# Attention and expert layer on one core: another start order, rows in a ring, one store to a slot

## The chip, the cores and the metric

The kernel runs on one core of one Trainium2 chip. The metric is the device time of one execution in microseconds (us), as the median of several runs. The engines are TensorE (PE, with its weight loads shown as PEld), VectorE (DVE), ScalarE (ACT), GpSimd (POOL) and SyncE (SP), which here only issues DMAs. TensorE's clock can be throttled; the profile shows the granted share.

## The reference

Two stages follow each other. The first is a gated linear attention over 768 steps for 4 batches of 8 heads, with head size 48; the second is an expert layer with 8 experts, of which each token uses one.

```python
f = 1.0 / (1.0 + np.exp(-f_logit))
for t in range(S):
    state = f[:, :, t, :, None] * state + np.einsum('bhd,bhe->bhde', k[:, :, t], v[:, :, t])
    y[:, :, t] = np.einsum('bhd,bhde->bhe', q[:, :, t], state)
...
x = attn_out.transpose(0, 2, 1, 3).reshape(B * S, H * D)      # 3072 tokens of 384
logits = x @ w_gate
expert_idx = np.argmax(logits, axis=1)
...                                                            # tokens go to their expert's rows in order
h = np.maximum(np.einsum('ecd,edf->ecf', disp, w1), 0.0)
y = np.einsum('ecf,efd->ecd', h, w2)
out[i] = gate_w[i] * y[expert_idx[i], pos[i]]
```

## The kernel before, in words

The 3072 tokens are 24 blocks of 128 (`NT`), six to a batch. Attention runs as a software pipeline over slots: slot n, from -4 to 24, issues on every engine the instructions that belong to several blocks at once. The order on all five engines is written out by hand here (`tc.manual_schedule`): each engine's queue holds its instructions in the order in which `slot` issues them, and an instruction that waits holds up what is behind it on its engine. Ahead of the slots stand constants and the first loads, which a planner orders.

For block n the steps are, with the lines of the profile:

- `load` (L198 to L217): DMAs of f, of k and q (one each, to two halves of the partitions of one tile), and of v. One load of f serves two blocks; "f 2" below is the load for blocks 4 and 5. k and q have three buffers, f three, v six.
- `sig(u)` (L344, ACT): the sigmoid of load u of f into `pf`. `sig(0)` is in two parts.
- `f_in` (L353, PE): transposes of `pf` into `psF`. `decay` and `decay_back` (L373 to L387, DVE): two scans over it, `Suf` and `Rq`.
- `kq_pad` (L394 on POOL, L396 on ACT from slot 7 on): copies k and q into a padded tile `kqp`. `kq_in` (L353, PE, then L402, DVE): transposes into `psT`, and the products with `Suf` and `Rq`, called `kT` and `qT`.
- `scores_pe` (L413, PE) and `scores_out` (L419, ACT, then L421, POOL): scores, their copy into `AT`, and the causal mask.
- `keys_pe` (L438, PE) and `keys_out` (L444, ACT): keys transposed back (`kn`). The last block of a batch has none.
- `inter` (L455), `update` (L475), `values` (L509): products with the carried state, for the state, and for the output. `state` (DVE) and `carry` (L495, POOL) make the next state `S`.
- `rows_pe` (L530, PE), `rows_copy` (L542, ACT) and `rows_parts` (L553, ACT): output rows of 384 values and parts of the eight logits, by a product with `identc`, which holds an identity and the gate weights. A row has 393 columns: values, logits and the token's number, which POOL copies in (L538). `rows` is a tile of six blocks with two buffers.

In slot 0 the sigmoid of f 2 stands ahead of the copies of block 1's scores on ACT. `update` takes its PSUM bank from the pool `psA` of two, in which both halves of the scores lie until ACT has copied them.

Choosing the expert and ranking go by groups of blocks (six, six, three, three, three, one, one, one). When a group is ranked, its blocks join `queue`, and `flush_scatter` issues one indirect DMA on POOL (L313) that stores the 128 rows of one block to `disp`, in HBM. A slot has two places for it: ahead of `update`, and behind `carry`; `SCATTERS` says how many a slot does (2 where it isn't listed). Blocks up to 14 are early: their rows of the first expert are loaded as `xg0` at the end of slot 19 (L930) and used from L708 on. From slot 5 on the first expert's weights are loaded and split in pieces between the attention's instructions; the experts' products (L744, L996, L1169) follow.

`keep_busy(m)` (L363) issues m products of the identity, whose result nobody reads: 10 ahead of the slots, 3 in slot -3, 7 in slot -2. The small constants are collected with `put_off` and made on POOL in slot -3 (L814). `late_constants` issues five small DMAs, the gate weights into `identc` and the capacity (L269, L270).

Of the kernel before, what the change touches and what calls it, by code (L numbers as in the profile page):

```python
# [28 lines left out]
def kernel(  # L29
# [45 lines left out]
    QUARTERS = {9: (0, 3), 12: (0, 1), 13: (1, 2), 14: (1, 2), 18: (2, 1), 19: (2, 1), 20: (2, 2)}  # L75
    SCATTERS = {9: 1, 10: 2, 11: 2, 12: 1, 15: 2, 16: 2, 17: 2, 18: 2, 19: 1, 20: 0}
    PAD_ACT = 7
# [135 lines left out]

    for nm, n in (("f", 0), ("kq", 0), ("f", 1), ("kq", 1), ("v", 0), ("kq", 2), ("f", 2)):
        load(nm, n)
        if (nm, n) == ("kq", 0):
            nc.sync.dma_start(loads["f", 0].rearrange("t h j d -> t h (j d)")[64:], pairs("f", 1, C))  # L217
# [18 lines left out]
    def put_off(op, *args, **kw):  # L236
        put_off_ops.append((op, args, kw))

    identc = const.tile([P, NP, XW], F32, name="identc")
    put_off(nc.gpsimd.memset, identc, 0.0)  # L240
# [15 lines left out]
    desc = const.tile([P, NE], F32, name="desc")  # L256
    put_off(nc.gpsimd.tensor_copy, desc, desc_i)
    tok_i = const.tile([P, N // C], I32, name="tok_i")
    put_off(nc.gpsimd.iota, tok_i, pattern=[[C, N // C]], base=-TOK0, channel_multiplier=1)
# [5 lines left out]
    def late_constants():  # L265
        gates_of = w_gate.rearrange("(a b s d) e -> b s d a e", b=2, s=2, d=D)
        for g in range(2):
            for b in range(2):
                nc.sync.dma_start(identc[64 * g : 64 * g + D, b::2, 2 * D :], gates_of[b, g ^ b])  # L269
        nc.sync.dma_start(cap_i, capacity.bitcast(I32).partition_broadcast(P))  # L270
    ohc = const.tile([P, NE], BF16, name="ohc")
# [133 lines left out]
    MS = (64, D)  # L405
    pus, ATs, kns, pys, yTs, marks, rows_of, parts_of = {}, {}, {}, {}, {}, {}, {}, {}

# [8 lines left out]
    def scores_out(n, pas):  # L416
        AT = abuf.tile([P, 2, NP, C], F32, name="AT")
        for s in range(2):
            nc.scalar.activation(AT[:, s], pas[s], AF.Copy)  # L419
# [104 lines left out]
    def rows_pe(n):  # L524
# [7 lines left out]
        return px  # L532

    def row_at(n):
        t, c = divmod(n, RT)
        if t not in rows_of:
            rows_of[t] = abuf.tile([P, RT, W], F32, name="rows")
            nc.gpsimd.tensor_copy(rows_of[t][:, :, DM + NE : W], tokid[:, n : n + RT].unsqueeze(2))  # L538
        return rows_of[t][:, c]

    def rows_copy(n, px):
        m = nc.scalar.activation(  # L542
            row_at(n)[:, :DM].rearrange("r (a d) -> r a d", a=NP), px[:, :, : 2 * D], AF.Copy
        )
        if n >= NT - 5:
            flush_scatter()
        marks[n].append(m)
# [7 lines left out]
    def group(g, m):  # L555
        t, c = divmod(g, RT)
        return parts_of[t][:, c : c + m], rows_of[t][:, c : c + m, DM : DM + NE]

# [21 lines left out]
    def sum_parts(g, m):  # L580
        t, c = divmod(g, RT)
        nc.vector.tensor_reduce(
            out=rows_of[t][:, c : c + m, DM : DM + NE],
            in_=parts_of[t][:, c : c + m].rearrange("r c a e -> r c e a"),
# [90 lines left out]

    def flush_scatter():
        if queue:
            n = queue.pop(0)
            late = n >= SPLIT
            ins = scatter(disp, ri_of.pop(n), row_at(n), NV * RPE - 1, ("disp", "late") if late else ("disp",))  # L680
            if not late:
                early_ins[:] = [ins]


# [85 lines left out]
    def loads_of(n):  # L770
        if n == -3:
            load("kq", 3)
            load("v", 1)
        elif n == -2:
            load("kq", 4)
            late_constants()
        elif n == -1:
            load("v", 2)
            load("f", 3)
            load("kq", 5)  # L780
        elif n >= 0:
# [11 lines left out]
    def slot(n):  # L793
# [16 lines left out]
        if fn and n < PAD_ACT:  # L810
            kq_pad(n + 3)
        while n == -3 and put_off_ops:
            op, args, kw = put_off_ops.pop(0)
            op(*args, **kw)  # L814
        while half:
# [5 lines left out]
        if n == -2:  # L821
            keep_busy(7)
        if n % 2 and fn and n not in (-3, 1, 9, 15):
# [21 lines left out]
        early_job(n, 1)  # L845
        if nxt and SCATTERS.get(n, 2):
            flush_scatter()
        if keyed:
# [14 lines left out]
        if keyed:  # L863
            carry(n)
        if nxt and SCATTERS.get(n, 2) > 1:
            flush_scatter()
        if fn and n >= 0:
# [28 lines left out]
        if prev and done and not tail:  # L896
            g, m = done
            if n - 1 >= NT - 2 * NCH:
                sum_parts(g, m)
                chosen[g] = choose(rows_of[g // RT][:, g % RT : g % RT + m], m, abuf, tallies[-1][:, 1 : m + 1]), m  # L900
            else:
# [103 lines left out]
    with tc.manual_schedule(  # L1005
# [7 lines left out]
    ):  # L1013
        keep_busy(10)
        nc.scalar.activation(warm, direv[:, :1], AF.Sigmoid)
# [399 lines left out]
```

## Time and profile before

| What | us |
|---|---|
| Median of 3 runs (389.15 to 390.94) | 390.06 |
| The profiled execution, its own time | 389.75 |
| Its span, first to last instruction | 387.7 |
| First scores (L413, block 0) start | 13.87 |
| First store of rows (L313) starts | 63.90 |
| Last of the 24 stores of rows starts | 149.19 |

Rows of the timeline show the start in us from the span's start, the length, the engine, the line, the operation with what it writes and reads, and in brackets the idle time of the engine before it and what ended that. Rows of the chain that ended last show start, length and what the chain went through. An x with a number counts the instructions merged into a row. A product of full-precision operands appears as two records.

### The profile page before, as it was taken

The numbers are of one execution on the slowest core, as the hardware profiler recorded it, in microseconds if no ns is written. First come the engines' busy times: TensorE is split into PE (matmuls) and PEld (weight loads), VectorE is DVE, ScalarE is ACT, GpSimd is POOL, SyncE is SP. The second block draws the span as 40 slices with busy tenths as digits, with TensorE's granted clock in tenths as the row PEclk, the third lists the DMA queues.
The fourth block names the chain that finished last, engine by engine and source line by source line (L and its number), as shares of the span: only waits on it lengthen the run. The fifth ranks groups of instructions, "written<-read, shape, count | busy, mean of one in ns | idle before, by whom it ended". The sixth has DMA issues, their size and how long they took to land.

```text
span 387.7 us, 10154 instructions
## 1 busy us (share of the span) xinstructions
PE 374.5 (97%) x4021; PEld 350.0 (90%) x4021; DVE 211.1 (54%) x482; ACT 200.7 (52%) x425; POOL 176.2 (45%) x251
## 2 busy tenths in 40 slices
PE   6899999999999999999999999999999999999993
PEld 6889889889988889998899989999999999999993
DVE  4798888879889758554844343325235235221310
ACT  3356677676877542462845552545463464462310
POOL 5655545766876643436164340280280271292001
PEclk9899999999999999999999999999999999999998
DMA  8999999898893322679476074166056136211001
GB/s 159 208 168 224 226 220 244 209 229 205 224 260 101 133 85 95 231 208 316 168 240 222 5 266 123 42 216 199 36 175 204 55 114 215 80 58 42 14 22 39
DMA packets 83322, 60.87 MB, mean 157 GB/s; under 512 B 65671, under 2 KB 77829, under 8 KB 83268
## 3 DMA queue, kind: packets, MB, share of 16 engines
q1 hardware_dynamic: 79476, 50.13, 50.0%
q0 software_dynamic: 3520, 9.92, 6.8%
q8 instruction: 33, 0.54, 0.6%
q14 instruction: 21, 0.17, 0.2%
q10 hardware_dynamic: 272, 0.10, 0.1%
HBM read 49.42 MB, written 11.43 MB: 157 GB/s over the span
## 4 chain that ended last, share of the span: by engine, by line
PE 82%; issue 9%; POOL 2%; ACT 2%; DVE 1%; DMA 1%; SPq 1%; POOLq 1%; DVEq 0%
PE psM L1169 14%; PE psA L744 12%; PE psM L744 11%; PE psM L996 9%; PE psA L413 6%; PE psA L530 5%; PE psY L509 5%; PE psT L353 3%; PE psY L455 3%; PE psA L475 2%; PE psT L1140 2%; PE psF L353 2%; PE psT L438 2%; PE psF L744 2%; POOL out_dram L313 1%
## 5 line engine op out<-in xcount | busy, mean ns | idle before, releaser
L313 POOL DMA_INDIRECT out_dram<-yo,g_ti x30 | 29.9, 998 | 100.9 <-ACT yo L1185 40.2
L143 POOL TENSOR_TENSOR w2l<-raw,w2h 128x768 fp32r<-128x768 f32 x28 | 51.2, 1854 | 38.7 <-ACT w2h L134 38.5
L751 DVE SCALAR_TENSOR_TENSOR hl<-psA,hh 128x224 fp32r<-128x224 f32 (+8 forms) x33 | 18.4, 559 | 49.0 <-ACT hh L750 49.0
L421 POOL TENSOR_SCALAR_AFFINE_SELECT AT<-AT 128x512 f32<-128x512 f32 x48 | 29.4, 635 | 24.1 <-ACT AT L419 24.1
L143 DVE TENSOR_TENSOR w1l<-raw,w1h 128x1024 fp32r<-128x1024 f32 x21 | 25.4, 1222 | 23.8 <-ACT w1h L134 23.6
L134 ACT ACTIVATE w1h<-raw 128x1024 fp32r<-128x1024 f32 x24 | 25.3, 1062 | 25.0 <-DMA raw<-in_moe_w_dram 24.9
L996 PE MATMUL psM<-w2h,hh 128*128 128x384 f32 (+2 forms) x112 | 37.6, 342 | 0.0
L996 PE MATMUL psM<-w2l,hh 128*128 128x384 f32 (+2 forms) x112 | 37.5, 338 | 0.0
L996 PE MATMUL psM<-w2h,hl 128*128 128x384 f32 (+2 forms) x112 | 37.4, 337 | 0.0
L751 DVE SCALAR_TENSOR_TENSOR hl<-psM,hh 128x224 fp32r<-128x224 f32 (+7 forms) x32 | 17.7, 562 | 30.9 <-ACT hh L750 30.9
L1169 PE MATMUL psM<-hh,w2h 128*128 128x440 f32 (+3 forms) x96 | 34.1, 355 | 0.0
L1169 PE MATMUL psM<-hl,w2h 128*128 128x440 f32 (+3 forms) x96 | 34.1, 355 | 0.0
L1169 PE MATMUL psM<-hh,w2l 128*128 128x440 f32 (+3 forms) x96 | 33.8, 352 | 0.0
L134 ACT ACTIVATE w2h<-raw 128x768 fp32r<-128x768 f32 x32 | 27.1, 846 | 10.1 <-DMA raw<-in_moe_w_dram 7.8
L373 DVE TENSOR_TENSOR_SCAN Suf<-psF,direv 112x511 f32<-112x511 f32 x24 | 29.1, 1210 | 4.6 <-PE psF L353 4.5
L419 ACT ACTIVATE AT<-psA 128x512 f32<-128x512 f32 x48 | 26.5, 618 | 8.3 <-PE psA L413 8.2
L413 PE MATMUL psA<-qT,kT 48*128 48x128 f32 x384 | 29.3, 282 | 1.0 <-DVE qT L402 1.0
L750 ACT ACTIVATE hh<-psA 128x224 fp32r<-128x224 f32 (+8 forms) x33 | 16.2, 491 | 27.2 <-PE psA L744 22.0
L744 PE MATMUL psM<-xh,w1h 128*128 128x480 f32 (+6 forms) x84 | 29.8, 354 | 0.0
L744 PE MATMUL psM<-xl,w1h 128*128 128x480 f32 (+6 forms) x84 | 29.7, 354 | 0.0
L744 PE MATMUL psA<-xh,w1h 128*128 128x480 f32 (+6 forms) x84 | 29.6, 353 | 0.0
L744 PE MATMUL psA<-xh,w1l 128*128 128x480 f32 (+6 forms) x84 | 29.4, 350 | 0.0
(237 smaller groups left out, 960.3 us busy)
## 6 DMA issues: line engine op xcount, KB each, us to landing
raw<-in_moe_w_dram SPq DMA_DIRECT2D x24, 512.0 KB
raw<-in_moe_w_dram SPq DMA_DIRECT2D x32, 384.0 KB
ld_kq<-in_k_dram SPq DMA_DIRECT2D x24, 192.0 KB
ld_kq<-in_q_dram SPq DMA_DIRECT2D x24, 192.0 KB
ld_v<-in_v_dram SPq DMA_DIRECT2D x24, 192.0 KB
ld_f<-in_f_logit_dram SPq DMA_DIRECT2D x11, 384.0 KB
xg<-disp SPq DMA_DIRECT2D x6, 589.5 KB
xg<-disp SPq DMA_DIRECT2D x3, 393.0 KB
```

What stands on the lines that cost most here:

```text
L134: return nc.scalar.activation(hi, raw, AF.Copy)
L143: engine.tensor_tensor(lo[cs], raw[cs], hi[cs].bitcast(F32), op=ALU.subtract)
L313: ins = nc.gpsimd.indirect_dma_start(out=dst, out_offset=bass.IndirectOffsetOnAxis(ap=idx, axis=0), in_=rows, in_offset=None, bounds_check ...
L373: nc.vector.tensor_tensor_scan(out=_view(Suf[:R], m - 1, [[-1, m]]), data0=_view(F, m, [[-1, m]]), data1=_view(direv[:R], m - 1, [[-1, m]] ...
L413: nc.tensor.matmul(pas[s][:, p], kTs[n][r, p], qTs[n][r, p], start=True, stop=True)
L419: nc.scalar.activation(AT[:, s], pas[s], AF.Copy)
L421: nc.gpsimd.affine_select(AT[:, s], AT[:, s], pattern=[[0, NP], [1, C]], compare_op=ALU.is_ge, fill=0.0, base=0, channel_multiplier=-1)
L509: nc.tensor.matmul(py[b][64 * g : 64 * g + m, a, :], vt[:, 2 * p + s, :m], AT[:, s, p, :], start=(first(n) and a == 0), stop=(a == NP // 2 ...
L744: nc.tensor.matmul(ph[:, :T], a[:, c, fs], x[:, c, :T], start=(n == 0), stop=(n == 3 * DT - 1))
L751: nc.vector.scalar_tensor_tensor(out=hl[:, :T], in0=ph[:, :T], scalar=0.0, in1=hh[:, :T].bitcast(F32), op0=ALU.max, op1=ALU.subtract)
L996: nc.tensor.matmul(py[:n], x[:, ks], a[:, ft], start=(ft == 0 and m == 0), stop=(ft == FT - 1 and m == 2))
L1169: nc.tensor.matmul(pys[c][:, :T], a[:, ft, cs], x[:, :T], start=(ft == 0 and n == 0), stop=(ft == FT - 1 and n == 2))
```

## The change

- `keep_busy` issues 7 products ahead of the slots, 5 in slot -3 and 3 in slot -2.
- `f_in(1)` moves from slot -3 to slot -2, behind the key transposes of block 0.
- Loads ahead of the slots: k and q of block 1 now come ahead of f 1, and f 2 is no longer among them. In slot -2 v 1 and f 2 are loaded (before: k and q of block 4), in slot -1 k and q of block 4, v 2, k and q of block 5, and f 3.
- `late_constants` stays in slot -2 and issues from ACT's queue, no longer from SP's.
- The constants up to `desc` are made ahead of the slots, the rest in slot -2.
- Rows lie in one ring of twelve blocks, made once, whose token numbers are copied in slot -2; from block 12 on each row gets its token number by a copy of its own.
- The place for stores ahead of `update` is gone. `SCATTERS` has mostly 1, and all stores of a slot stand behind `carry`. In slots 15, 17, 19 and 21 (`AHEAD`) one more is issued between the copy of the scores and the mask, and waits for that copy.

```diff
-    SCATTERS = {9: 1, 10: 2, 11: 2, 12: 1, 15: 2, 16: 2, 17: 2, 18: 2, 19: 1, 20: 0}
+    SCATTERS = {9: 1, 10: 1, 11: 1, 12: 1, 13: 1, 14: 1, 15: 1, 16: 2, 17: 1, 18: 1, 19: 1, 20: 0}
+    AHEAD = (15, 17, 19, 21)
...
-    for nm, n in (("f", 0), ("kq", 0), ("f", 1), ("kq", 1), ("v", 0), ("kq", 2), ("f", 2)):
+    for nm, n in (("f", 0), ("kq", 0), ("kq", 1), ("f", 1), ("v", 0), ("kq", 2)):
...
     put_off(nc.gpsimd.tensor_copy, desc, desc_i)
+    later_ops(put_off_ops)
...
-                nc.sync.dma_start(identc[64 * g : 64 * g + D, b::2, 2 * D :], gates_of[b, g ^ b])
-        nc.sync.dma_start(cap_i, capacity.bitcast(I32).partition_broadcast(P))
+                nc.scalar.dma_start(identc[64 * g : 64 * g + D, b::2, 2 * D :], gates_of[b, g ^ b])
+        nc.scalar.dma_start(cap_i, capacity.bitcast(I32).partition_broadcast(P))
...
         for s in range(2):
-            nc.scalar.activation(AT[:, s], pas[s], AF.Copy)
+            copied = nc.scalar.activation(AT[:, s], pas[s], AF.Copy)
+        if n - 1 in AHEAD:
+            flush_scatter(copied.ins)
...
+    ring = abuf.tile([P, 2 * RT, W], F32, name="rows", bufs=1)
+
     def row_at(n):
-        t, c = divmod(n, RT)
-        if t not in rows_of:
-            rows_of[t] = abuf.tile([P, RT, W], F32, name="rows")
-            nc.gpsimd.tensor_copy(rows_of[t][:, :, DM + NE : W], tokid[:, n : n + RT].unsqueeze(2))
-        return rows_of[t][:, c]
+        return ring[:, n % (2 * RT)]
...
     def rows_copy(n, px):
+        if n >= 2 * RT:
+            nc.gpsimd.tensor_copy(row_at(n)[:, DM + NE : W], tokid[:, n : n + 1])
...
         if n == -3:
             load("kq", 3)
+        elif n == -2:
+            late_constants()
             load("v", 1)
-        elif n == -2:
+            load("f", 2)
+        elif n == -1:
             load("kq", 4)
-            late_constants()
-        elif n == -1:
             load("v", 2)
+            load("kq", 5)
             load("f", 3)
-            load("kq", 5)
...
-        while n == -3 and put_off_ops:
-            op, args, kw = put_off_ops.pop(0)
-            op(*args, **kw)
+        if n == -2:
+            later_ops(put_off_ops)
+            nc.gpsimd.tensor_copy(ring[:, :, DM + NE : W], tokid[:, : 2 * RT].unsqueeze(2))
...
         if n == -2:
-            keep_busy(7)
+            f_in(1)
+            keep_busy(3)
...
-        if nxt and SCATTERS.get(n, 2):
-            flush_scatter()
         if keyed:
             pu = update(n)
...
         if keyed:
             carry(n)
-        if nxt and SCATTERS.get(n, 2) > 1:
-            flush_scatter()
+        if nxt:
+            for s in range(SCATTERS.get(n, 2)):
+                flush_scatter()
...
-        if n in (-4, -3):
-            f_in(n + 4)
+        if n == -4:
+            f_in(0)
         if n == -3:
-            keep_busy(3)
+            keep_busy(5)
...
-        keep_busy(10)
+        keep_busy(7)
```

More of the change, by code (lines that the diff above doesn't have):

```diff
@@ L237, in put_off, with later_ops @@
         put_off_ops.append((op, args, kw))
+    def later_ops(ops):
+        while ops:
+            op, args, kw = ops.pop(0)
+            op(*args, **kw)
     identc = const.tile([P, NP, XW], F32, name="identc")
@@ L405 @@
     MS = (64, D)
-    pus, ATs, kns, pys, yTs, marks, rows_of, parts_of = {}, {}, {}, {}, {}, {}, {}, {}
+    pus, ATs, kns, pys, yTs, marks, parts_of = {}, {}, {}, {}, {}, {}, {}
     def scores_pe(n):
@@ L532, in rows_pe, with rows_at @@
         return px
+    ring = abuf.tile([P, 2 * RT, W], F32, name="rows", bufs=1)
     def row_at(n):
-        t, c = divmod(n, RT)
-        if t not in rows_of:
-            rows_of[t] = abuf.tile([P, RT, W], F32, name="rows")
-            nc.gpsimd.tensor_copy(rows_of[t][:, :, DM + NE : W], tokid[:, n : n + RT].unsqueeze(2))
-        return rows_of[t][:, c]
+        return ring[:, n % (2 * RT)]
+    def rows_at(g, m):
+        c = g % (2 * RT)
+        return ring[:, c : c + m]
     def rows_copy(n, px):
+        if n >= 2 * RT:
+            nc.gpsimd.tensor_copy(row_at(n)[:, DM + NE : W], tokid[:, n : n + 1])
         m = nc.scalar.activation(
@@ L556, in group @@
         t, c = divmod(g, RT)
-        return parts_of[t][:, c : c + m], rows_of[t][:, c : c + m, DM : DM + NE]
+        return parts_of[t][:, c : c + m], rows_at(g, m)[:, :, DM : DM + NE]
     def choose_sum(g, m):
@@ L582, in sum_parts @@
         nc.vector.tensor_reduce(
-            out=rows_of[t][:, c : c + m, DM : DM + NE],
+            out=rows_at(g, m)[:, :, DM : DM + NE],
             in_=parts_of[t][:, c : c + m].rearrange("r c a e -> r c e a"),
@@ L674, with flush_scatter @@
     queue, early_ins, slot_now, ri_of = [], [], {"n": 0}, {}
-    def flush_scatter():
+    def flush_scatter(behind=None):
         if queue:
@@ L680, in flush_scatter @@
             ins = scatter(disp, ri_of.pop(n), row_at(n), NV * RPE - 1, ("disp", "late") if late else ("disp",))
+            if behind is not None:
+                tc.add_manual_dep(
+                    ins,
+                    behind.name,
+                    mybir.DependencyInfo(mybir.DependencyClass.Sync, mybir.DependencyReason.DATA),
+                    reason="not during the transposes",
+                )
             if not late:
@@ L899, in slot @@
                 sum_parts(g, m)
-                chosen[g] = choose(rows_of[g // RT][:, g % RT : g % RT + m], m, abuf, tallies[-1][:, 1 : m + 1]), m
+                chosen[g] = choose(rows_at(g, m), m, abuf, tallies[-1][:, 1 : m + 1]), m
             else:
```

## The prediction, made blind

> **What bounds the kernel now.** I read the page's head and chain first, to see which engine sets the end.
>
> ```profile
> PE 374.5 (97%) x4021; PEld 350.0 (90%) x4021; DVE 211.1 (54%) x482; ACT 200.7 (52%) x425; POOL 176.2 (45%) x251
> PE 82%; issue 9%; POOL 2%; ACT 2%; DVE 1%; DMA 1%; SPq 1%; POOLq 1%; DVEq 0%
> ```
>
> PE is busy for 97% of the span and holds 82% of the chain that ended last. Time is therefore gained only where PE waits, and a microsecond taken off another engine is worth nothing while PE has work queued. The change touches two stretches: the first 21 us, and slots 9 to 22, where rows are scattered. Next I read the chain of the first stretch, then the timeline of the instructions on it.
>
> ```profile
> 3.19 4.43 DMA ld_f<-in_f_logit_dram
> 7.64 0.85 ACT pf L344
> 10.34 1.03 PE psT L353 x13
> 11.37 2.57 PE psA L363 x14
> 16.45 0.68 DVE qT L402
> ```
>
> L363 is the product of the identity. A batch of 14 records, 2.57 us, lies on the chain: real work stands behind filler there. The chain then goes through DVE, to block 1's qT at 16.45 to 17.13.
>
> ```profile
> 1.83 4.57 PE L363 MATMUL psA<-ident 128*128 128x128 f32 x20 [1.83 <-POOL ident masks.py:199]
> 4.17 0.84 ACT L344 ACTIVATE pf<-ld_f 64x768 f32<-64x768 f32 x1 [1.12 <-DMA ld_f<-in_f_logit_dram]
> 6.34 0.66 PE L353 MATMUL psF<-ident,pf 64*112 64x64 f32 x8
> 6.84 0.82 POOL L394 COPY kqp<-ld_kq 128x768 f32<-128x768 f32 x1 [3.06 <-DMA ld_kq<-in_q_dram]
> 7.03 1.22 DVE L373 TENSOR_TENSOR_SCAN Suf<-psF,direv 112x511 f32<-112x511 f32 x1 [4.55 <-PE psF L353]
> 8.50 1.22 DVE L387 TENSOR_TENSOR_SCAN Rq<-psF,d 112x512 f32<-112x512 f32 x1
> 9.28 0.84 ACT L344 ACTIVATE pf<-ld_f 128x768 f32<-128x768 f32 x1 [0.80 <-DMA ld_f<-in_f_logit_dram]
> 10.03 0.19 POOL L814 CAST desc<-desc_i 128x8 f32<-128x8 int32 x1
> 16.10 3.35 SPq L269 DMA_DIRECT2D identc<-in_moe_w_gate_dram  x4
> 16.51 0.86 ACT L344 ACTIVATE pf<-ld_f 128x768 f32<-128x768 f32 x1
> 17.48 0.82 POOL L394 COPY kqp<-ld_kq 128x768 f32<-128x768 f32 x1 [0.52 <-DMA ld_kq<-in_q_dram]
> 18.43 1.09 ACT L419 ACTIVATE AT<-psA 128x512 f32<-128x512 f32 x2 [1.06 <-PE psA L413]
> 19.08 0.48 PEld L475 LDWEIGHTS psA<-ld_v,kn 128*64 128x64 f32 x15 [0.34 <-ACT AT L419]
> 20.57 0.84 PE L438 MATMUL psT<-ident,kT 64*128 64x64 f32 x8
> ld_kq<-in_k_dram SPq DMA_DIRECT2D x24, 192.0 KB
> ld_v<-in_v_dram SPq DMA_DIRECT2D x24, 192.0 KB
> ld_f<-in_f_logit_dram SPq DMA_DIRECT2D x11, 384.0 KB
> ```
>
> Bracketed is the idle time before an instruction and what ended it. A wait that a DMA ended dates that landing: f's second pair of blocks (f 1) by 9.28, q of block 3 by 17.48.
>
> **Part 1, the start, step by step.** The identity products fall from 10, 3 and 7 to 7, 5 and 3 (two records each). At 4.57/20 = 0.23 us a record, 14 records end at 5.0, just as the first sigmoid does (4.17 + 0.84). Block 0's F transposes (0.66) then end at 5.7 instead of 7.0, and its two scans (7.03 to 9.72, so 2.69) end at 8.4. Ten records take PE to 8.0 at the latest, kqp is there at 7.66, and kT and qT of block 0 (1.03 of transposes, then 0.68 each) end at 10.4. Block 1's F transposes now stand behind block 0's key transposes, still inside DVE's time. Block 1's scans (2.69) and its kT and qT (1.36) end at 14.5, against 17.13 before. By this chain alone the start would be 2.6 us earlier.
>
> What is late next is f's third load (f 2, blocks 4 and 5). Its sigmoid (16.51, 0.86) stands on ACT in slot 0, ahead of the copies of block 1's scores (18.43), and the update of block 0 waits for the first copy (19.08). Before, f 2 is issued ahead of block 3's k and q; afterwards it comes behind them and behind v 1. Between f 1 (9.28) and q 3 (17.48) there landed k 1, q 1, v 0, k 2, q 2, f 2, k 3 and q 3: 1728 KB in 8.2 us, 211 KB per us. Afterwards v 1 (192 KB, 0.91 us) must land too before f 2 is complete, and no other order moves these bytes sooner: 18.4 us. Sigmoid until 19.25, first copy 0.65 (18.43 to 19.08), update at 19.9: 0.8 us later than before. Block 1's key transposes took 0.84 us at 20.57, held up by block 2's qT, where 0.46 is usual (row at 106.87 below); that 0.38 us goes, since DVE is now early. Net **+0.4 us**. Bounds: -2.6 if f 2 were in time; the upper bound is the clock's, a rival below.
>
> The four gate loads and the capacity move from SP's queue to ACT's. SP's loads get back 3.35 us and more of issue time. ACT pays as much, between its sigmoid at 7.64 and the score copies of block 0, behind which the sigmoid of f 1 and those copies queue; all of this ends before 18.4, so f 2 covers it. If f 2 were early, it would cost up to 3.35 us there. [...]
>
> POOL's constants in two parts: the first part, up to desc, ran from 7.66 (end of the pad at 6.84) to 10.22, so 2.6 us, and fits into POOL's 3.06 us of idle time before 6.84. The rest goes behind block 1's pad, where PE doesn't wait for POOL. Cost nothing; if the first part overran, kqp of block 0 would move by the overrun, which f 2 again covers.
>
> **Part 2, the scatter.** Slots are marked on the chain by L413, one per slot.
>
> ```profile
> 26.83 0.96 PE psA L413 x14
> 60.65 0.95 PE psA L413 x15
> 82.07 0.95 PE psA L413 x15
> 92.26 0.95 PE psA L413 x15
> 118.50 1.25 PE psA L413 x16
> 106.87 0.46 PE L438 MATMUL psT<-ident,kT 64*128 64x64 f32 x8
> 106.87 0.97 POOL L313 DMA_INDIRECT disp<-rows,ri  x1 [0.30 <-issue]
> 108.51 0.61 ACT L444 ACTIVATE kn<-psT 128x256 f32<-128x256 f32 x2 [1.05 <-PE psA L413]
> 112.71 0.28 PE psA L413 x2
> 107.33 1.20 PE psA L413 x14
> ```
>
> Slots 9 to 19 last 57.85 us (60.65 to 118.50). Slots 13 and 14 issue no scatter and last 5.10 each (82.07 to 92.26); slots 2 to 8 last 4.83 (26.83 to 60.65). So the nine slots with scatters cost between 57.85 - 11 x 5.10 = 1.8 and 57.85 - 11 x 4.83 = 4.7 us together. How they cost is seen at 106.87: the scatter starts with the key transposes, which end at 107.33, and ACT, idle, copies them only at 108.51. That slot lasts 5.38 (107.33 to 112.71), 0.28 over 5.10 and 0.55 over 4.83.
>
> Afterwards each slot from 9 to 19 has one store behind the carry, slots 13 and 14 too, and 15, 17 and 19 one more ahead of the mask, behind the copy of the scores; 16 has two. A store behind the carry starts close to the next key transposes, like the one at 106.87. Nine of the eleven slots that follow begin with key transposes. If each pays as that one, it is 9 x 0.28 = 2.5 against 1.8 by the one base (+0.7), and 9 x 0.55 = 5.0 against 4.7 by the other (+0.3). Against that, doubles fall from six slots (10, 11, 15 to 18) to four: two pairs less at 0.28 are -0.6. I take **0**. Bounds: -4.7 if none is felt, +0.7.
>
> The ring lets a row be rewritten once its own store has landed, twelve slots back; nothing waits there before or after. The token numbers take nine copies more on POOL, each about as small as desc's at 10.03 (0.19), 1.7 us in all on an engine busy for 45%: no cost. The store ahead of the mask waits for ACT's copy, as the mask does; behind it queue two masks and the carry, and the values product of the next slot waits for those, some 2 us off. Cost nothing.
>
> The last early store leaves slot 19 behind the carry, some 2 us later than before, and with it the load of the first expert's rows.
>
> ```profile
> 116.65 0.99 POOL L313 DMA_INDIRECT disp<-rows,ri  x1 [0.16 <-issue]
> 119.38 0.37 SPq L930 DMA_DIRECT2D xg<-disp  x1
> 125.95 0.44 PE L708 MATMUL psF<-ident,xg 128*128 128x128 f32 x2
> ```
>
> From store to load took 2.73, from load to use 6.57; a load at 121.4 leaves 4.5 us, just the 4.43 that a load of f took from issue to landing with others ahead of it (3.19 on the chain). No cost, with little to spare; an overrun would be paid by PE.
>
> **Sum.** +0.4 + 0 = +0.4. The profiled execution took 389.75 (span 387.7), 0.31 under the median of 390.06; against the median: **390.5 us**.
>
> **Rivals.**
>
> *The stores are no longer felt* (faster). For it: slots 13 and 14 are short, and a single store may fall beside nothing urgent. Against: 106.87. Part 2 then gives -1.8 to -4.7, middle -3.2, so with +0.4: 390.06 - 2.8 = 387.3.
>
> *f 2 does not gate* (faster). For it: SP is 3.35 us ahead. Against: the byte count. The full 2.6 are gained at the start: 387.5.
>
> *The clock falls* (slower).
>
> ```profile
> 6.00:10.00 4.00, 2.46 (x25) 2.09 (x23) 2.66 (x4) 1.56 (x2) 2.89 (x10) 0.95 1.28 216
> 10.00:13.00 3.00, 3.00 (x26) 2.65 (x26) 1.59 (x3) 0.12 (x1) 2.46 (x24) 0.50 1.32 221
> 16.00:20.00 4.00, 2.82 (x67) 2.58 (x63) 3.96 (x7) 2.46 (x6) 2.69 (x5) 1.00 0.94 156
> ```
>
> PE was busy for 2.46 of 4 us (61%), then the granted clock was 0.50 for some 3.4 us, although PE was then full. Afterwards PE has nothing between block 2's transposes (about 17.1) and 19.9. If a stretch like 6 to 10 there falls to 61% or less, the clock halves as slots 0 and 1 begin, and 3.4 us at half speed cost 1.7: +2.1 in all, 392.2. Against: from 16 to 20 PE was busy for 2.82 of 4 us (70%) and the clock stayed at 1.00. [...]
>
> *The ring ties its rows together* (no spread): if a row's copy waited for another row's store, each would cost some of 2.7 us; slower, little chance.
>
> **How the numbers follow.** Chances: the forecast 0.45 (389.0 to 391.9), stores not felt 0.28, f 2 no gate 0.07, clock 0.17, ring 0.03. A change of 0.5%, 1.95 us, is about what can be told from none: faster is below 388.1, slower above 392.0. Faster: most of the first rival and half of the second, with the forecast's own edge, 0.32; slower: two thirds of the clock's, the ring's and an edge, 0.20; same 0.48. The range reaches to the middle of the first rival's gains and beyond the clock: 386.6 to 392.8.
>
> **What would show it.** Right: the sigmoid at about 18.4 ended by a DMA of f; the update of block 0 at about 19.9; L413 of slot 1 some 0.4 us later than 21.41; slots 13 and 14 no longer 5.10; kn copied over 1 us behind its transposes in most slots. Wrong: that sigmoid earlier than 17; slots 9 to 19 together under 56 us; a granted clock of 0.5 after 19 us; PE idle before L708.

## The result and the profile after

The changed kernel takes **392.04 us** (median of 20 runs, 390.12 to 395.26); the kernel before, run beside it on the same chip, 389.94 (20 runs, 386.81 to 391.82). The ratio is 1.0061, 95% interval 1.0038 to 1.0085: slower by 0.6%. 390.5 was predicted. The profiled execution after took 394.49 us with a span of 392.5, against 389.75 and 387.7 before; the differences of the traces below are between these two. It was one of the longer of its runs, and a second profile, further down, has a smaller loss at the start.

First the start. The chain that ended last, of the kernel after, from 7 us on (start, duration, what):

```profile
7.33 5.98 DMA ld_kq<-in_k_dram
13.33 0.60 SPq L204
13.97 1.68 SPq L199
15.70 5.23 DMA ld_f<-in_f_logit_dram
21.01 0.84 ACT pf L351
21.85 0.50 ACT AT L426
22.39 0.98 PE psA L484 x13
32.28 0.96 PE psA L420 x14
```

The chain no longer goes through the identity products and DVE. It goes through loads: block 2's keys (issued at 7.33), whose landing SP waits for before it issues block 3's q (L204 at 13.33), v 1 (L199), the third f load (f 2), the sigmoid of blocks 4 and 5 (L351), the first copy of block 1's scores (L426), and the update of block 0 (L484) at 22.39, which stood at 19.08 before. The scores of slot 2 are at 32.28; the same row before is at 26.83. The start has lost 5.45 us. The timeline of the same stretch:

```profile
21.01 0.84 ACT L351 ACTIVATE pf<-ld_f 128x768 f32<-128x768 f32 x1 [5.28 <-DMA ld_f<-in_f_logit_dram]
22.39 0.98 PE L484 MATMUL psA<-ld_v,kn 128*64 128x48 f32 x15 [4.42 <-ACT AT L426]
23.28 1.93 PE L518 MATMUL psY<-AT,ld_v 128*64 128x128 f32 x15
```

ACT waited 5.28 us for f 2 and PE 4.42 us for ACT. Busy time and clock by stretch, of the kernel after (columns: PE, PEld, DVE, ACT, POOL busy, granted clock, DMA share, GB/s), show what followed:

```profile
14.00:18.00 4.00, 2.99 (x75) 2.74 (x71) 3.04 (x6) 1.58 (x4) 2.84 (x4) 1.00 0.61 135
18.00:21.00 3.00, 0.00 (x0) 0.00 (x0) 1.99 (x3) 0.00 (x0) 0.00 (x0) 0.99 1.26 245
21.00:28.00 7.00, 5.61 (x71) 5.28 (x72) 2.92 (x5) 3.23 (x8) 2.50 (x4) 0.52 1.08 210
```

The first of these stretches in the kernel before:

```profile
14.00:18.00 4.00, 3.02 (x68) 2.92 (x70) 3.46 (x6) 2.31 (x5) 2.54 (x4) 1.00 1.32 224
```

PE did nothing from 18 to 21, and then the granted clock was 0.52 on average over 7 us. Two losses stand one behind the other: the wait for f 2, and slots 0 and 1 at half speed after it. f 2 is issued only at 15.70, behind SP's wait until 13.3 (7.33 + 5.98), and between 14 and 18 only 135 GB/s move, where the kernel before has 224.

Now the slots with stores. Their marks on the chain after:

```profile
65.85 0.95 PE psA L420 x15
101.05 1.06 PE psA L420 x15
112.87 1.00 PE psA L420 x15
```

Slot 9 starts at 65.85, slot 16 at 101.05 and slot 18 at 112.87. By the first score product of each slot, slots 9 to 19 take 56.94 us (57.86 before). Slots 10, 11 and 12 are down to 4.31, 4.81 and 4.75 (5.60, 5.15 and 5.41 before); slots 13 and 14, which now have stores, take 5.37 and 5.56 (5.17 and 5.03); slot 17 takes 7.14 (5.09) and gives most of the gain back. From slot 20 to the end it is 269.8 us after and 269.4 before. So 5.45 lost at the start, 0.25 gained in slots 2 to 8, 0.92 gained in slots 9 to 19 and about 0.4 lost behind them make the 4.7 us between the spans.

### The profile page after: what moved, and what is told of

Its sections match the earlier page's. It is cut to its first block, busy times and chain, and to the rows that moved or that the text cites. A ratio compares the mean times of both kernels' runs of the same rounds, so it can differ in the third digit from the quotient of the medians.

```text
span 392.5 us, 10149 instructions
## 1 busy us (share of the span) xinstructions
PE 375.4 (96%) x4011; PEld 351.1 (89%) x4011; DVE 212.6 (54%) x482; ACT 201.6 (51%) x425; POOL 178.9 (46%) x260
## 4 chain that ended last, share of the span: by engine, by line
PE 70%; issue 9%; DMA 9%; POOL 3%; SPq 2%; ACT 2%; DVE 2%; POOLq 1%; DVEq 0%; ACTq 0%
PE psM L1189 14%; PE psA L763 10%; PE psM L763 8%; PE psM L1016 5%; PE psY L518 5%; PE psA L420 5%; PE psA L539 5%; DMA raw<-in_moe_w_dram 4%; PE psY L464 3%; PE psA L484 2%; PE psT L360 2%; PE psT L447 2%; DMA disp<-zero,fill_at 2%; PE psT L1160 2%; PE psF L763 2%
## 5 line engine op out<-in xcount | busy, mean ns | idle before, releaser
L770 DVE SCALAR_TENSOR_TENSOR hl<-psA,hh 128x224 fp32r<-128x224 f32 (+8 forms) x33 | 18.4, 559 | 49.4 <-ACT hh L769 49.4
L320 POOL DMA_INDIRECT disp<-rows,ri x24 | 25.5, 1061 | 13.3 <-issue 4.3
```

What stands on the lines that cost most here:

```text
L320: ins = nc.gpsimd.indirect_dma_start(out=dst, out_offset=bass.IndirectOffsetOnAxis(ap=idx, axis=0), in_=rows, in_offset=None, bounds_check ...
L770: nc.vector.scalar_tensor_tensor(out=hl[:, :T], in0=ph[:, :T], scalar=0.0, in1=hh[:, :T].bitcast(F32), op0=ALU.max, op1=ALU.subtract)
```

## The experiments

The theory after this reading: f 2's landing sets the update of block 0, because its sigmoid stands on ACT ahead of block 1's score copies; the half clock follows from PE's idle time in that wait; and the stores are mostly no longer felt, except where several fall into one slot. The rivals: the loads as such are what is late, so that another load takes f 2's place; the clock falls for another reason; the stores cost the time.

The runs came on two chips, called here the faster (385.84 for the kernel before) and the third (390.59 and 390.07). Whether the third is the first one again is not on record. The table gives the chip by the median of the kernel before on it, the ratio to that kernel with its interval, and, from each trace, the start of slot 2 and the length of slots 9 to 19 and of slot 17 (first score product to first score product, us).

| run | before | ratio | slot 2 at | slots 9-19 | slot 17 |
|---|---|---|---|---|---|
| kernel before | 389.94 | 1 | 26.51 | 57.86 | 5.09 |
| kernel after | 389.94 | 1.0061 (1.0038-1.0085) | 31.96 | 56.94 | 7.14 |
| f 2 early | 385.84 | 1.0018 (0.9994-1.0043) | 27.21 | 54.71 | 5.46 |
| PE filled in the wait | 385.84 | 1.0096 (1.0062-1.0129) | 28.83 | 54.71 | 5.47 |
| start alone | 385.84 | 1.0076 (1.0044-1.0108) | 31.33 | 53.85 | 5.03 |
| stores alone | 385.84 | 1.0036 (1.0013-1.0060) | 26.92 | 54.72 | 5.49 |
| before, again | 390.59 | one run, 391.15 us | 26.61 | 56.58 | 5.08 |
| after, again | 390.59 | 1.0048 (1.0022-1.0073) | 29.52 | 57.11 | 7.22 |
| sigmoid in slot 1 | 390.59 | 0.9934 (0.9899-0.9968) | 25.25 | 59.60 | 8.74 |
| constants later | 390.59 | 1.0008 (0.9980-1.0036) | 30.08 | 57.68 | 7.30 |
| sigmoid in slot 1, again | 390.07 | 0.9938 (0.9906-0.9970) | 25.63 | 56.68 | 5.85 |
| the same, stores of before | 390.07 | 0.9956 (0.9932-0.9980) | 24.29 | 57.15 | 5.09 |
| the same, slot 17 thinned | 390.07 | 0.9972 (0.9944-1.0000) | 25.27 | 56.73 | 5.30 |
| the same, no stores in 16-18 | 390.07 | 1.0155 (1.0114-1.0195) | 24.74 | 58.43 | 4.84 |

### f 2 early

```
-    for nm, n in (("f", 0), ("kq", 0), ("kq", 1), ("f", 1), ("v", 0), ("kq", 2)):
+    for nm, n in (("f", 0), ("kq", 0), ("kq", 1), ("f", 1), ("v", 0), ("kq", 2), ("f", 2)):
...
             load("v", 1)
-            load("f", 2)
```

> The changed kernel, with the third f load (blocks 4 and 5) put back at the end of the six loads ahead of the slots. Theory (f gate): the update of block 0 waits for that load alone, and the half clock from 20.95 to 27.77 us follows from TensorE's idle time in that wait. Then the first sigmoid of slot 0 no longer waits for it, the update of block 0 starts between 17 and 20 us instead of 22.39, the scores of slot 2 start at 26 to 28 us instead of 31.96, and the kernel takes 386.5 to 388.5 us (0.990 to 0.997 of the kernel before). Rival (loads are one queue: what comes first delays the rest): the pads of blocks 3 and the values of block 1 land some 2.4 us later and take the gate's place; slot 2 starts at 30 us or later, and the time stays at 391 to 393. Rival (stores cost it): the start gains, and the time still stays at 391 or more.

Timeline and stretches of this run:

```profile
16.80 0.84 ACT L351 ACTIVATE pf<-ld_f 128x768 f32<-128x768 f32 x1 [1.94 <-DMA ld_f<-in_f_logit_dram]
18.18 0.98 PE L484 MATMUL psA<-ld_v,kn 128*64 128x48 f32 x15 [1.89 <-ACT AT L426]
13.00:18.00 5.00, 2.84 (x48) 2.45 (x48) 4.39 (x7) 3.06 (x7) 2.41 (x7) 0.76 1.20 211
18.00:21.00 3.00, 2.82 (x34) 2.49 (x36) 1.66 (x5) 0.61 (x2) 2.35 (x4) 0.50 0.87 197
```

The update of block 0 follows f 2 to the front: 18.18 instead of 22.39, and slot 2 starts at 27.21. Both are inside what the theory gave, and no pad or value load took f 2's place. The ratio of 1.0018 is above the expected 0.990 to 0.997. Two things are left. The sigmoid still waited 1.94 us for f 2, and the clock still fell, but not by that wait: by the clock records of the trace it fell at 15.61, before PE's pause of 1.89 us began, and the longest pause ahead of it is this one of 1.59 us:

```profile
13.44 0.66 PE L360 MATMUL psF<-ident,pf 64*112 64x64 f32 x16 [1.59 <-ACT pf L351]
```

And the stores of the change cost on this chip, as the run with the stores alone shows.

### PE filled in the wait

```
+        if n == 0:
+            keep_busy(20, psY)
         if cur:
             inter(n)
```

> The changed kernel, with 20 more products that nobody reads in slot 0, ahead of the intermediate products, so that TensorE is not idle while it waits for the sigmoid of blocks 4 and 5. The wait itself stays. Theory (f gate, the clock falls because of the idle stretch): the update of block 0 stays at 22.4 us, the clock stays at full speed from 14 us on, the identity products, transposes and scores of slots 0 and 1 run at full speed, slot 2 starts 1.5 to 2.2 us sooner (about 30 us), and the time is 389.8 to 390.8. Rival (the clock is not what costs, the chain behind the update is on VectorE and ScalarE): the clock stays up and slot 2 starts within 0.5 us of 31.96, time 391.5 to 392.5. Rival (the half clock comes from elsewhere, the 61% busy stretch ahead of it): the clock falls all the same, time 392 or more.

```profile
16.83 3.51 PE L370 MATMUL psY<-ident 128*128 128x128 f32 x30
21.73 0.61 PE L484 MATMUL psA<-ld_v,kn 128*64 128x48 f32 x15 [1.40 <-ACT AT L426]
22.23 1.05 PE L518 MATMUL psY<-AT,ld_v 128*64 128x128 f32 x15
```

The wait stays, and the clock does not fall: a batch of 15 values products takes 1.05 us here and 1.93 in the kernel after. The run with the start alone, on the same chip, has the same start without the filler; its update of block 0 is at 21.61 and its slot 2 at 31.33. Here these are 21.73 and 28.83, so the half clock costs **2.5 us**. The rivals (the clock is not what costs; the clock falls all the same) are out. The time shows no gain: 1.0096, with the stores of the change, against 1.0076 in the start alone, which has those of the kernel before and is 2.5 us later at slot 2. The two intervals overlap, and in the traces the stores take 1.8 us back in slots 9 to 20 (54.71 + 5.86 against 53.85 + 4.94).

### The start alone

The rows tiles, the stores and their two places are those of the kernel before; the rest is the change.

> The start of the change alone (fewer products at first, order of loads, constants in two parts), with the rows tiles, the stores and their places of the kernel before. Theory (the start costs 5.4 us to slot 2, the stores give 1.2 us back between slots 2 and 20): 393 to 395.5 us, 1.008 to 1.014 of the kernel before, and slower than the whole change by 1 us. Rival (the start's loss is made up by itself between slots 2 and 20, the stores do nothing): the same time as the whole change, 392. Rival (the stores cost the time): 390 or less.

PE's wait in this run:

```profile
21.61 0.98 PE L481 MATMUL psA<-ld_v,kn 128*64 128x48 f32 x15 [5.08 <-ACT AT L425]
```

The ratio of 1.0076 is just under the expected 1.008 to 1.014, and the start lost is the same as in the kernel after (slot 2 at 31.33). But slots 9 to 19 take only 53.85 us, with the same stores that stand in the kernel before with 57.86.

### The stores alone

The ring, the token copies and the store places of the change, on the start of the kernel before.

> The stores of the change alone (ring of rows, one place behind the carry, the three stores behind the score copy), on the start and the loads of the kernel before. Theory (a store behind the carry is felt in few slots): slots 9 to 19 take 56.5 to 57 us instead of 57.86, slot 17 with its four stores stays near 7 us, and the kernel takes 388.3 to 389.3 us, 0.996 to 0.999 of the kernel before. Rival (the prediction's: the stores only move their stall): 389.9, slots 9 to 19 at 57.8. Rival (the shorter slots 2 to 20 of the changed kernel came from its late start, work having been piled up ahead): slots 9 to 19 at 57.8 or more and 390 or more.

All three theories missed: the slots are shorter than any of them had it (54.72), and yet the kernel is slower, 1.0036. On this chip the stores of the kernel before cost less still: the start alone has 53.85 in slots 9 to 19 and 4.94 in slot 20, the stores alone 54.72 and 5.87, 1.8 us more. Most of the 1.8 us can be read in the traces: with the stores of the change PE waits in slots 14, 17 and 20 for `tally`, a step of the ranking, 0.27, 0.25 and 0.78 us, and in the start alone it doesn't. In slot 20 the step of the ranking on POOL ahead of `tally` starts only at 119.45, behind a store (117.58 to 118.60) and two other steps, and `tally` itself takes 0.96 us (0.48 in the start alone):

```profile
120.94 0.19 PE L675 MATMUL psA<-tally,onesb 128*128 128x16 bf16 x2 [0.78 <-DVE tally L584]
```

Not all of the 1.0036 need be the stores', for slot 3 takes 6.47 us in this trace, with the loads of the kernel before, and 5.09 and 5.64 in the two traces of that kernel, of which none is from this chip. So whether the store places gain or lose depends on something that differs between the chips. The next two runs looked for it.

### The kernels before and after, again

> The kernel before, unchanged, for a profile on the same chip as the next three runs: in the profile first shown its slots 9 to 19 took 57.86 us, where the run with the changed start and these same stores took 53.85 on another chip, whose times of the kernel before are 4 us shorter. Theory (whether the stores of the kernel before hold the handovers up differs from chip to chip, and that is the 4 us): where this kernel takes 386 us its slots 9 to 19 take 54 us, where it takes 390 us they take 58. Rival (the changed start frees the slots behind it of the stores' stall): 57 us or more on either chip.

> The changed kernel, unchanged, on the same chip as the kernel before and the runs behind it. Theory (the two parts add up: the start costs 4.4 us to slot 2, the stores 1.4 us more where those of the kernel before are not felt): 1.010 to 1.013 of the kernel before on a chip on which that takes 386 us, slots 9 to 19 at 54.7; 1.004 to 1.009 on a chip on which it takes 390, slots 9 to 19 at 57. Rival (the stores cost the same on every chip): 1.006 on either.

On this third chip, where the kernel before takes 390.59, its slots 9 to 19 take 56.58 us (58 was expected). With the changed start and the same stores they take 57.15 on the same chip (a run further down). So the start doesn't free them, and the rival is out; 53.85 belongs to the chip. The same instructions of slot 9 on the faster chip (start alone), and then on the third, the slower one (sigmoid in slot 1, stores of before):

```profile
68.26 0.89 PE L536 MATMUL psA<-identc,yT 112*64 112x104 f32 x15
68.47 1.19 POOL L319 DMA_INDIRECT disp<-rows,ri  x1 [0.22 <-issue]
69.20 0.49 ACT L548 ACTIVATE rows<-psA 128x384 f32<-128x384 f32 x1 [0.80 <-PE psA L536]
```

```profile
61.33 0.89 PE L536 MATMUL psA<-identc,yT 112*64 112x104 f32 x15
61.55 1.19 POOL L319 DMA_INDIRECT disp<-rows,ri  x1 [0.22 <-DVE qT L408]
62.92 0.49 ACT L548 ACTIVATE rows<-psA 128x384 f32<-128x384 f32 x1 [1.44 <-PE psA L536]
```

The rows products end at 69.15 (68.26 + 0.89), and ACT copies them 0.05 us later, in the middle of the store. On the slower chip they end at 62.22, and ACT starts 0.70 us later, 0.18 us after the store's instruction (61.55 + 1.19) is over. All four traces of the faster chip have slots 9 to 19 at 53.9 to 54.7, all ten of the others at 56.6 to 59.6. In slots 9 to 19 of the four traces of the faster chip no wait of ACT or DVE that ended during a store was answered over 0.3 us late; in the kernel after four were. So on the first and the third chip a store held some handovers up (0.70 us here), but not all: in slot 17 of the kernel after the rows products end at 111.61, in the middle of a store (111.11 to 112.10), and ACT, idle till then, copies them at 111.71.

The kernel after is slower on this chip too, by less: 1.0048. The theory of two parts that add up had 1.004 to 1.009 here. The rival (the same cost on every chip, 1.006) lies in the interval too, so this run doesn't part the two. The change was not run whole on the faster chip; its parts there, 1.0076 and 1.0036, would add to 1.011.

### The sigmoid of blocks 4 and 5 in slot 1

```
-        if n == 0:
+        if n == 1:
             sig(2)
```

> The changed kernel, with the sigmoid of blocks 4 and 5 in slot 1 instead of slot 0, so that the score copies of block 1 on ScalarE no longer stand behind the third f load. That load still lands at 20 to 21 us. Theory (f gate by ScalarE's order): the update of block 0 starts at 17.5 to 18.5 us instead of 22.39, TensorE is idle for less than 3 us in slots 0 and 1, slot 2 starts at 25 to 27 us instead of 31.96, and the time is 4.5 to 6 us below the changed kernel's. Rival (the keys of block 1 or the pads of block 3 hold slot 0 at the same place): update of block 0 at 20 us or later, slot 2 at 29 or later, less than 3 us gained. Rival (the wait moves to slot 1, whose score copies stand behind the sigmoid now): slot 0 takes 4 us and slot 1 8 or more.

The chain that ended last, of this run:

```profile
14.40 0.68 DVE qT L409
18.92 0.44 PE psT L447 x7
20.37 0.88 ACT pf L351
25.57 0.96 PE psA L420 x14
```

and two instructions of its timeline:

```profile
17.05 0.61 PE L484 MATMUL psA<-ld_v,kn 128*64 128x48 f32 x15 [0.20 <-ACT AT L426]
20.37 0.87 ACT L351 ACTIVATE pf<-ld_f 128x768 f32<-128x768 f32 x1
```

f 2 lands hardly sooner (19.14, in the records of its transfers; 19.40 in the kernel after on this chip). But the update of block 0 is at 17.05, PE waited 0.20 us for it, and the sigmoid in slot 1 waits for no load. The clock stays up through the start (in the repeated run it was half from 14.9 to 18.3 us, and slot 2 starts 0.4 us later). Slot 2 starts at 25.25, against 29.52 in the kernel after and 26.61 in the kernel before on this chip. The ratio is **0.9934** (0.9899 to 0.9968), and 0.9938 (0.9906 to 0.9970) when the run was repeated: 1.1% below the kernel after on the same chip by the ratios (0.9934 / 1.0048 = 0.989), and a version that beats both kernels. By the medians it is 3.5 us (392.5 - 389.02), less than the 4.5 to 6 expected: the kernel after lost less at the start here than in the first profile, and slot 17 takes 8.74 us in this trace. One line of order on ACT decided the sign. The same line was not moved in the kernel before; there ACT waits 1.06 us for PE behind that sigmoid (the row at 18.43 in the prediction), so it held nothing up.

### The constants later

```
         elif n == -2:
-            late_constants()
             load("v", 1)
...
             load("v", 2)
+            late_constants()
             load("kq", 5)
```

and the five loads on SP's queue again.

> The changed kernel, with the five loads of small constants issued on SyncE in slot -1 ahead of the keys of block 5, as in the kernel before, instead of on ScalarE in slot -2. Theory (SyncE waits at each issue for the landing of an earlier transfer, and the five constants lengthen that): the third f load is issued at 12 to 14 us instead of 15.70 and lands at 17.5 to 19.5 instead of 20.93, the update of block 0 starts 1.5 to 3 us sooner, and the time is 1.5 to 4 us below the changed kernel's, more if the clock stays up. Rival (the bytes ahead of it set when f 2 lands, as the prediction had it): it lands at 18.4 with the constants in either place, that is, at 20 or later here too where the changed kernel has 20.9; no gain over 0.5 us. Rival (the constants land too late for the first rows): TensorE waits in slot 1 ahead of the first rows product.

Chain and stretches:

```profile
12.57 7.49 DMA ld_f<-in_f_logit_dram
14.00:18.00 4.00, 3.48 (x53) 3.31 (x51) 2.52 (x5) 1.58 (x4) 2.88 (x5) 1.00 1.19 226
18.00:21.00 3.00, 1.81 (x26) 1.60 (x23) 2.52 (x5) 0.85 (x2) 0.00 (x0) 1.00 0.88 133
```

The kernel after on the same chip:

```profile
14.00:18.00 4.00, 2.27 (x47) 2.02 (x47) 3.96 (x8) 0.58 (x3) 2.51 (x4) 1.00 0.79 173
```

SP is freed: it issues f 2 at 12.57, where the kernel after has 14.51 on this chip (15.70 in the first profile), and between 14 and 18 the transfers move 226 GB/s instead of 173. The traces show how. In the first profile of the kernel after, the loads issued on SP and ACT carry eight semaphores in turn. With the five constants taking their turns on ACT, block 3's q gets the semaphore of block 2's keys and waits for it: the keys' last update comes at 13.31, the issue at 13.33. With the constants later, by the same turns, it gets that of a part of f issued at 3.18 and goes out at 11.23. f 2 still lands only at 20.06 (12.57 + 7.49), where the same chip's run of the kernel after had 19.40. By the updates of its semaphore a load lands in 16 shares (f 2 in the first profile from 19.07 to 20.93). The first share of f 2 was complete at 17.16 here (18.55 there), the last 2.9 us later (0.85 there). So the constants did hold SP and the bytes up; but the landing that the sigmoid waits for is the last share's (20.93 in the first profile, with the sigmoid at 21.01), and that was no sooner. The expected 17.5 to 19.5 did not come; 20 or later, the rival's landing, did, though not by its reason, since the bytes were early. PE does not wait ahead of the first rows product in slot 1, so the third rival is out. The median is 0.3% below that of the kernel after (391.2 against 392.5), but the intervals overlap, so no difference can be told. Slot 2 is late in this trace (30.08) for another reason: by its clock records PE first reaches full speed at 24.77, and this execution was the longest of its twelve (392.44).

### Four kernels on one start

> The changed kernel with the sigmoid of blocks 4 and 5 in slot 1, a second time, as the base of the three runs behind it on the same chip. Expected: 0.990 to 0.997 of the kernel before, slot 2 at 25 to 26 us; slot 17, with four stores, at 5.5 us on a chip on which the kernel before takes 386 us and at 7 to 9 on one on which it takes 390.

> The start of the change with the sigmoid of blocks 4 and 5 in slot 1, and the rows tiles, stores and store places of the kernel before. Theory (the stores of the change move the stall into slot 17 and take more from slot 20 on than they save): slots 9 to 19 shorter than with the stores of the change by 0.5 to 2.5 us (54 to 57.5 against 54.7 to 59.6), slot 17 at 5.1, and the time 0.5 to 2 us below that of the same start with the stores of the change. Rival (the places of the change are the better ones, as slots 10, 12, 16 and 18 of the first profile say): 0.5 to 1.5 us above it.

> The changed kernel with the sigmoid in slot 1 and the stores of slots 16 to 19 spread anew: one behind the carry of slot 16 instead of two, none behind the score copies of slot 17, two behind the carries of slots 18 and 19. Slot 17 then has two stores in it instead of four; the sum is the same. Theory (four stores in one slot make its stall): slot 17 at 4.7 to 5.5 us, slots 18 to 20 longer by 0.5 to 1 us together, the time 1 to 3 us below that of the changed kernel with the sigmoid in slot 1 where its slot 17 takes 7 us or more, the same where that takes 5.5. Rival (TensorE's pauses in slot 17 come from elsewhere, such as the weight pieces that are loaded and split there): slot 17 stays at 7 us or more.

> The changed kernel with the sigmoid in slot 1 and no store behind the carries of slots 16, 17 and 18 at all: three are issued behind the carry of slot 15 and six behind that of slot 19. It shows what slots 17 and 18 take without stores, and what stores in a heap cost. Theory: slot 17 at 4.7 to 5.1 us, slot 18 at 4.75, slots 16 and 20 long by 1 to 4 us each, and the whole no better than the run with the stores spread. Rival (the stall of slot 17 isn't the stores'): slot 17 at 7 us or more as in the base.

The edits to the store places, on the start with the sigmoid in slot 1:

```
 stores of the change:   9 to 15: 1   16: 2   17: 1   18: 1   19: 1   ahead of the mask: 15, 17, 19, 21
 slot 17 thinned:        9 to 15: 1   16: 1   17: 1   18: 2   19: 2   ahead of the mask: 15, 19, 21
 no stores in 16 to 18:  9 to 14: 1   15: 3   16 to 18: 0     19: 6   ahead of the mask: 21
```

*The stores of before* give 0.9956 against 0.9938: the intervals overlap, so on this chip the store places make no difference that can be told. The gain expected did not come; the medians (388.47 against 387.48) lie as the rival had it, but not clear of the noise.

*No stores in 16 to 18.* Slots 17 and 18 take 4.84 and 4.75, so slot 17's length is the stores'. It is not their number alone: with the stores of before slot 17 has three and takes 5.09. The three in a heap behind slot 15's carry make slot 16 8.31 long, and the six behind slot 19's make slot 20 12.31 long, more than the 1 to 4 us expected. In both the clock halves as well, for 3.41 us from 98.04 and 6.83 us from 121.94. Slot 16, timeline:

```profile
93.38 1.01 POOL L320 DMA_INDIRECT disp<-rows,ri  x1 [0.22 <-issue]
94.70 0.98 POOL L320 DMA_INDIRECT disp<-rows,ri  x1 [0.30 <-issue]
95.98 0.98 POOL L320 DMA_INDIRECT disp<-rows,ri  x1 [0.30 <-issue]
93.91 1.12 PE L420 MATMUL psA<-qT,kT 48*128 48x128 f32 x16
95.21 0.88 PE L360 MATMUL psT<-ident,kqp 64*112 64x64 f32 x16 [0.18 <-issue]
97.91 0.91 PE L464 MATMUL psY<-qT,S 48*64 48x128 f32 x10 [1.04 <-issue]
98.05 1.08 ACT L426 ACTIVATE AT<-psA 128x512 f32<-128x512 f32 x2 [2.12 <-remote]
98.19 0.69 DVE L409 TENSOR_TENSOR kT<-psT,Suf 112x512 f32<-112x512 f32 x1 [3.02 <-remote]
```

The stores follow each other at 1.3 us, and ACT, DVE and PE stand still side by side: ACT's score copy for 2.12 us and DVE for 3.02, though PE's scores ended at 95.03 (93.91 + 1.12) and its transposes at 96.09 (95.21 + 0.88). PE itself pauses in the middle of a batch, for 1.04 us with nothing awaited that the profile shows. So here it isn't that POOL's own work queues behind the stores: handovers between the other engines are late, and ACT and DVE go on only 1.1 to 1.2 us after the third store's instruction (95.98 + 0.98) is over.

The same in slot 17 of the kernel after, with four stores in it:

```profile
105.79 1.02 POOL L320 DMA_INDIRECT disp<-rows,ri  x1 [0.22 <-issue]
107.12 0.98 POOL L320 DMA_INDIRECT disp<-rows,ri  x1 [0.30 <-issue]
108.67 1.02 POOL L320 DMA_INDIRECT disp<-rows,ri  x1 [0.19 <-issue]
109.32 0.46 PE L464 MATMUL psY<-qT,S 48*48 48x128 f32 x4 [0.33 <-issue]
110.05 0.48 PE L464 MATMUL psY<-qT,S 48*64 48x128 f32 x8 [0.26 <-issue]
111.11 0.99 POOL L320 DMA_INDIRECT disp<-rows,ri  x1 [0.17 <-issue]
```

"One to a slot" in the code is not one to a slot on POOL. POOL runs late there, so slot 16's two stores come at the start of slot 17, and the one ahead of the mask and its own behind them. In the first run with the sigmoid in slot 1 the clock halved in that slot too, as it did in no other trace with four stores there:

```profile
105.00:108.60 3.60, 3.60 (x45) 3.24 (x42) 3.56 (x7) 1.31 (x3) 1.85 (x4) 0.53 0.90 291
```

Slot 17 takes 8.74 us there. In the second run of the same kernel POOL was not late, slot 17 had two stores and took 5.85.

*Slot 17 thinned* does what it should in that slot (5.30), and slots 19 and 20 take it back (5.90 and 7.10, against 5.56 and 5.45 in the base), 2.0 us where 0.5 to 1 was expected. At 0.9972 it is no better than the base: moving the stores about among the last slots moves the stall.

## Why the prediction was right, and where not

**The number and the sign.** 390.5 was forecast and 392.04 measured, within the range (386.6 to 392.8), and 2.10 us above the kernel before beside it, where the forecast had +0.4. That is just past the forecast's own edge of "slower", 392.0, and the interval of the ratio leaves out "no change". The range held because it had been drawn past the clock rival's 392.2, not by the sum. That 392.04 lies so near the rival's figure is partly luck: the start lost 5.45 and 2.9 us in the two pairs of traces, not 2.1, and later slots gave some back.

**Identity products and DVE's chain: about right in size, covered as said.** The sum had -2.6 by this chain alone. With f 2's sigmoid out of the way, slot 2 comes 1.0 to 2.3 us sooner than in the kernel before on that chip (24.29 to 25.63 in five traces, against 26.61). Block 1's qT ends at 15.08 (14.40 + 0.68), where 14.5 was predicted and 17.13 stood before. In the first profile of the kernel after it is 16.21, with PE at half speed until 14.12.

**f 2 gates: right in mechanism, mis-sized.** The sigmoid ended by a DMA of f, the copy behind it and the update behind that are as described. The term that failed is f 2's landing: 18.4 was worked out, and 20.93 came. The estimate was a count of bytes at 211 KB per us, as if the queue were full to the end and all shares landed at once. Neither holds. SP waited for block 2's keys to land, issued f 2 at 15.70, and the transfers moved 135 GB/s between 14 and 18 (the kernel before: 224), so that the first share of f 2 was complete at 19.07 only; and the last share came 1.86 us behind the first, where in the kernel before the two are 0.81 apart. With SP free (constants later) the bytes were early, first share at 17.16, and the tail was 2.9 us. Over the nine other traces with this order of loads f 2 landed between 19.1 and 20.3, never at 18.4. Why the tail is longer than before stays open. A second issuer did not save SP time here: on the third chip SP issued f 2 at 14.51 with the constants on ACT's queue and at 12.57 with them on its own, behind f 2. The prediction had SP 3.35 us ahead.

**The clock: the rival that came, on top.** It was given 0.17, for a gap of 2.8 us (17.1 to 19.9). Since f 2 was 2.5 us later than worked out, the gap became 4.42, and the clock halved in slots 0 and 1: one of the prediction's own signs of being wrong, a granted clock of 0.5 after 19 us. The price was put at 1.7 for 3.4 us, and 2.5 was measured for 6.83 us. It halved for 6.83 us in two of the three traces that have this wait with nothing to fill it and PE at full speed ahead of it, and in the third for 3.41. The two were treated as separate cases, where one brought the other: a later f 2 was a longer gap, and with PE filled in it the clock did not fall. In the gap of 4.42 us the clock fell after 2.98 (17.97 to 20.95). Other falls came after shorter pauses: the longest pause of PE in the 6.8 us ahead of them is 1.54 us in the kernel before, 1.59 in the run with f 2 early, and 0.42 in slot 17 of the first run with the sigmoid in slot 1. What decides a fall stays open: PE's busy share does not either, with 2.31 of 3.41 us ahead of the fall in that slot 17, and 2.02 of 3.41 us, from 19.60 on, without a fall in the run with PE filled.

**The stores: 0, right in the sum and wrong in the reason.** Slots 9 to 19 changed by -0.92 on the first chip and +0.53 on the third. But the step behind it, that a store behind the carry is paid at the next key transposes in most slots, failed: slots 10, 11 and 12 were 4.31 to 4.81, free of any stall. Only slots 13 and 14 paid as predicted (5.37 and 5.56), the keys ahead of them copied 0.42 and 0.62 us behind their transposes; over 1 us, the sign named, came in no slot. What balanced it was not counted at all: POOL's lateness, which put four stores into slot 17. That the sum came out near 0 is luck. Under 56 us, the mark for "wrong", was reached only on the chip on which stores hold little up.

**Costs set at nothing.** In the profile of the kernel after, no wait of PE is traced to POOL's constants, the ring or the token copies. The constants' move to ACT was covered there as said, but it is what held SP up. The load of the first expert's rows (issued at 126.16 after) reached PE in time for its transposes at 130.25.

## What to carry to other kernels

Before a load is moved later, look not only for who needs its data but also for who stands behind the instruction that waits for it: here one sigmoid, not needed for another slot, held the score copies of block 1, and moving it by one slot was worth 1.1%, more than the 0.7% that the whole change gains with it. When work is taken off a filled stretch, count the wait behind it together with the clock that the idle time costs, since here the wait (5.08 us in the start alone) brought a second loss of 2.5 us. And the indirect stores cost here by where they fell (slot 17 on the third chip: 7.22 us with four of the change, 5.09 with three in the places of before, 4.84 with none): see on POOL's own timeline where they fall, not in the slot where the code puts them, and measure on more than one chip before store places are tuned.

## What the runs showed of the hardware that was not expected

- While an indirect store ran on GpSimd, some handovers between other engines were late: 0.70 us at one store, 2 to 3 us over three in a row, with a pause of 1.04 us inside a PE batch. Others were not (0.10 us in slot 17 of the kernel after). On the faster chip the same instructions were not held up (0.05 us), and the kernel before is 4 us shorter there. What differs between the chips stays open.
- When the clock first reached full speed varied: in the three profiles with the start of the kernel before at 6.2 to 7.1 us by the clock records, in the eleven with the changed start at 4.7 to 24.8 (14.1 in the kernel after). Half-speed stretches between full-speed ones lasted 3.41 us (from 9.63 in the kernel before) or 6.83 us (from 20.95 in the kernel after). In the run with the constants later PE was busy for 8.00 of the 8 us from 6 to 14 and stayed at half speed. What sets the moment, and how much of the spread of the times from run to run is this, was not tested.
- Where a trace has no clock record yet, the clock column shows 1.00, while the durations show half: in the run with the constants later, a batch of 16 score products took 2.08 us at 16.88, where it took 1.12 at full speed (93.91 in the run with no stores in 16 to 18). Read the clock from durations at the start.
